# Retention and GLU feed-forward on one core: GLU blocks of 512 columns instead of 384

## The chip, the cores and the metric

The kernel runs on one core of a Trainium2 chip. The metric is the device time of one execution, in microseconds; the median of several executions is compared.

## What is computed

The reference is a retention layer (attention with a decaying mask and without softmax) followed by a feed-forward layer with a sigmoid gate. There are 8 batches and 8 heads, with 576 positions of 64 elements.

```python
scores = scale * np.matmul(q, k.transpose(0, 1, 3, 2))
gamma = 1.0 - 2.0 ** (-5.0 - np.arange(H))
Dmat = np.where(rel >= 0, gamma[:, None, None] ** rel[None, :, :], 0.0)
attn_out = np.matmul(scores * Dmat[None], v)
x = attn_out.transpose(0, 2, 1, 3).reshape(B * S, H * D)      # 4608 x 512
gate = 1.0 / (1.0 + np.exp(-(x @ w_gate)))                    # 4608 x 1536
out = (gate * (x @ w_val)) @ w_out                            # 4608 x 512
```

All inputs and the output are float32 in memory; the kernel multiplies in bfloat16 and accumulates in float32.

## The kernel before, in words

The retention is computed chunk by chunk with a running state. Its result stays on chip as xT (512 x 4608, transposed, with one column for each token), and the feed-forward reads it from there. The columns of xT come in the order in which the steps are computed. The first 768 columns come from three pairs of chunks that a start-up part handles by its own code (lines 624 to 784), together with the feed-forward of columns 0 to 511.

After that the work is in STEPS (line 68), numbered from 0: one step is one chunk of one batch, 128 columns, or 64 for the last chunk of a batch (a short step). Steps 0 to 6 end at columns 896, 1024, 1088, 1152, 1280, 1408 and 1536; steps 2 and 3 are short, steps 4, 5 and 6 are the first three chunks of batch 2.

A step is made ready by loads_to and casts_to, which call the functions at lines 98 to 107 and 244 to 292: SyncE loads v, k and q (line 105), GpSimd multiplies k and q by decay tables and writes them to qk_nat in bfloat16 (lines 252 and 262), SyncE issues a transposing DMA that makes T from qk_nat (line 289), and GpSimd casts v into vbd (line 273). qk_nat, vbd and T exist four times. On each queue these stand in the order load of step s + 1, transpose of step s, load of step s + 2 and so on; the casts of step s + 3 are emitted with the QK phase of step s (LEAD_CAST).

TensorE then works a step off in phases: st0, qk, st1, pv, each of 4 to 16 matmuls of 64 columns. "st" (line 432) adds a half chunk to the state, which DVE copies to sbd (line 438). "qk" (line 399) needs T; DVE multiplies its result with a triangular mask (line 401). "pv" (lines 418 and 420) gives the columns of xT, which ACT copies (line 422). A short step has only qk and pv, and its qk stands ahead of the pv of the step before it. The list of all phases is "order".

The feed-forward runs in BLOCKS of columns. In each block and for each of 12 slices of the 1536 hidden columns, TensorE multiplies xT with a slice of w_gate and one of w_val, four matmuls each (line 495), ACT takes the sigmoid (line 519; 509 in blocks of 256 columns), and DVE multiplies (523; 511), which gives gv. Then 12 output matmuls for each 128 columns (line 561) and a copy by ACT (line 538) give the result, which SyncE stores (line 533) nine tiles late. The PSUM pool for the GLU and output tiles has three buffers of 512 float32 columns.

The two streams are interleaved by hand. ffn_units yields after each small group of matmuls: in a block of 256 columns after each slice, in wider blocks after each gate half and each value half, and in the output part after the 4th, 8th and 12th matmul of each tile. The main loop (line 789 on) then calls advance, which runs as many attention phases as the share of the block's work that is done asks for. By the end of a block, all steps whose columns the next block reads must be done: last_step and upto (lines 581 to 586) turn the next block's last column into a place in "order". The share is spread over the block without its last 6144 columns of matmul work (3 x 2048). What stands in each engine's queue is thus the order in which the program emits it.

Of the kernel before, what the change touches and what calls it, by code (L numbers as in the profile page):

```python
# [16 lines left out]
def kernel(  # L17
# [22 lines left out]
    NT, DM = out.shape  # L40
# [489 lines left out]
    def leave():  # L530
        r, ob = stores.pop(0)
        for p0, r0, w in rows(r, P):
            nc.sync.dma_start(out[r0:r0 + w, :], ob[p0:p0 + w])
# [47 lines left out]
    def upto(s):  # L581

        return order.index(("pv", s)) + 1

    def last_step(t1):
        return max(s for s in range(NS) if at_col[s] < t1)
# [196 lines left out]
        nc.vector.memset(t, 0.0)  # L783
    casts_to(1)

    BLOCKS = [(512, 256), (768, 256)] + [(t, 384) for t in range(1024, 2560, 384)]
    BLOCKS += [(t, 512) for t in range(2560, NT, 512)]
    pieces = 0
    for w, (t0, n) in enumerate(BLOCKS):
        nxt = BLOCKS[w + 1] if w + 1 < len(BLOCKS) else None  # L790
        end = upto(last_step(nxt[0] + nxt[1])) if nxt else len(order)
# [4 lines left out]
        for cols in ffn_units(t0, n):  # L796
            gone += cols
            pieces += 1
            if stores and (nxt is None or w + 2 == len(BLOCKS) and pieces % 4 == 0):
                leave()  # L800
# [33 lines left out]
```

## Time and profile before

| what | us |
|---|---|
| median of 7 runs | 337.09 (336.85 to 337.69) |
| profiled execution | 338.22 |
| its span, first to last instruction | 336.4 |
| TensorE matmul busy | 328.7 |
| weight loads busy | 184.3 |
| GpSimd busy | 185.8 |
| ACT busy | 167.8 |
| DVE busy | 164.8 |

The profile is of one execution, which took 338.22 us; all times inside it count from the first instruction of its span. Groups of instructions by line and shape that touch the change (count, busy time, mean of one):

| line, engine, what | shape | count | busy us | mean ns |
|---|---|---|---|---|
| 495 PE, gate half | 128x256 | 96 | 14.4 | 273 |
| 495 PE, gate half | 128x384 | 192 | 39.1 | 326 |
| 495 PE, gate half | 128x512 | 192 | 49.3 | 379 |
| 519 ACT, sigmoid | 128x384 | 48 | 23.6 | 491 |
| 519 ACT, sigmoid | 128x512 | 48 | 28.7 | 597 |
| 523 DVE, product | 128x384 | 48 | 26.6 | 555 |
| 523 DVE, product | 128x512 | 48 | 33.0 | 688 |
| 561 PE, output | 128x512 | 372 | 85.5 | 379 |

The value half of line 495 has the same counts and times as the gate half. The mean duration of a matmul contains its latency, and matmuls overlap, so a duration is longer than the spacing of two in a row. In the timeline of this execution the blocks start at 55.65 (column 512), 74.42 (768) and 92.47 us (1024).

### The profile page before, as it was taken

The page shows a single profiled execution, that of the slowest core. Times are in us where ns is not written, and L with a number is a line of the kernel's source. Part 1 is how long each engine was busy: PE and PEld are TensorE (multiplying, and loading weights), DVE is VectorE, ACT ScalarE, POOL GpSimd, SP SyncE. Part 2 cuts the span into 40 slices and gives each one's busy share as a digit, 9 for nine tenths or more (in the row PEclk, how much of TensorE's full clock was granted, in tenths as well). Part 3 has the DMA queues.
Part 4 walks back from the last instruction along what each step waited for, and adds up shares of the span by engine and source line. Part 5 has one row for each costly group of instructions (what it writes and reads, how often), then busy time and mean ns, then how long its engine had stood idle before and what let it go on. Part 6 is the DMA issues. An engine that isn't in the chain of part 4 may idle for free.

```text
span 336.4 us, 7396 instructions
## 1 busy us (share of the span) xinstructions
PE 328.7 (98%) x2784; PEld 184.3 (55%) x2784; DVE 164.8 (49%) x328; ACT 167.8 (50%) x345; POOL 185.8 (55%) x327
## 2 busy tenths in 40 slices
PE   7999998999999999999999999999999999999996
PEld 3544545869666566556566655544555455444443
DVE  5745765627466455536346635642664156503320
ACT  6545635537665556355456655445545455233321
POOL 5565669688968898783448976482567500000000
PEclk9999999999999999999999999999999999999999
DMA  7999996899999999999975999599773850020002
GB/s 205 312 372 367 312 250 129 141 229 193 184 211 196 185 193 218 225 237 214 230 137 113 183 244 199 105 222 255 135 143 82 244 212 2 0 95 33 0 31 95
DMA packets 164100, 60.00 MB, mean 178 GB/s; under 512 B 144480, under 2 KB 156000, under 8 KB 164064
## 3 DMA queue, kind: packets, MB, share of 16 engines
q1 hardware_dynamic: 163920, 59.39, 83.6%
q8 instruction: 22, 0.36, 0.5%
q10 hardware_dynamic: 144, 0.13, 0.1%
q14 instruction: 14, 0.11, 0.1%
HBM read 37.75 MB, written 9.44 MB: 140 GB/s over the span
## 4 chain that ended last, share of the span: by engine, by line
PE 87%; DMA 5%; POOL 4%; DVE 2%; issue 1%; ACT 0%; SPq 0%; POOLq 0%; DVEq 0%
PE h L495 46%; PE op L561 24%; PE hg L610 3%; PE hv L610 3%; DMA wo<-in_moe_w_out_dram 2%; PE pv L420 2%; PE qk L399 2%; PE pv L418 2%; DMA T<-qk_nat 2%; PE st L432 2%; POOL qk_nat L252 1%; DMA k32p<-in_k_dram 1%; PE op L551 1%; DVE ptp L335 1%; PE idle L159 1%
## 5 line engine op out<-in xcount | busy, mean ns | idle before, releaser
L495 PE MATMUL h<-xT,wg_sb 128*128 128x384 bf16 (+2 forms) x480 | 102.8, 337 | 0.2 <-DVE gv L523 0.2
L495 PE MATMUL h<-xT,wv_sb 128*128 128x384 bf16 (+2 forms) x480 | 102.8, 337 | 0.0
L252 POOL TENSOR_TENSOR qk_nat<-k,ktab 64x256 bf16<-64x256 f32 x120 | 73.5, 612 | 41.8 <-PE st L432 27.2
L523 DVE TENSOR_TENSOR gv<-g,h 128x384 bf16<-128x384 bf16 (+1 forms) x96 | 59.7, 621 | 71.7 <-PE h L495 56.4
L561 PE MATMUL op<-wo_sb,gv 128*128 128x512 bf16 x372 | 85.5, 379 | 0.0
L519 ACT ACTIVATE g<-h 128x384 bf16<-128x384 f32 (+1 forms) x96 | 52.2, 544 | 64.9 <-PE h L495 58.3
L438 DVE CAST sbd<-st 64x256 bf16<-64x256 f32 x104 | 43.7, 420 | 45.1 <-PE st L432 42.9
L495 PEld LDWEIGHTS <-wg_sb 128*128 128x128 bf16 x480 | 43.7, 98 | 31.4 <-issue 0.4
L495 PEld LDWEIGHTS <-wv_sb 128*128 128x128 bf16 x480 | 44.1, 98 | 29.0 <-issue 0.4
L273 POOL CAST vbd<-v 64x256 bf16<-64x256 f32 x120 | 47.6, 397 | 15.8 <-PE pv L420 11.2
L561 PEld LDWEIGHTS <-gv 128*128 128x128 bf16 x372 | 34.4, 98 | 36.3
L538 ACT COPY ob<-op 128x512 f32<-128x512 f32 x33 | 19.3, 586 | 47.5 <-PE op L561 42.8
L283 ACT CAST vs<-v 64x256 bf16<-64x256 f32 x104 | 41.9, 403 | 1.6
L262 POOL TENSOR_TENSOR qk_nat<-q,qtab 128x512 bf16<-128x512 f32 (+1 forms) x34 | 35.4, 1042 | 2.6
L422 ACT CAST xT<-pv 128x512 bf16<-128x512 f32 (+1 forms) x34 | 18.2, 534 | 18.1 <-PE pv L420 18.0
L401 DVE TENSOR_TENSOR pt<-qk,tri 128x512 bf16<-128x512 f32 (+1 forms) x34 | 21.2, 625 | 6.1 <-PE qk L399 5.8
L420 PE MATMUL pv<-pt,vbd 128*128 128x64 bf16 x240 | 18.0, 193 | 0.0
L432 PEld LDWEIGHTS <-qk_nat 128*128 128x128 bf16 x208 | 13.2, 98 | 8.8
L511 DVE TENSOR_TENSOR gv<-g,h 128x256 bf16<-128x256 bf16 x24 | 10.0, 421 | 14.7 <-ACT g L509 14.4
L418 PE MATMUL pv<-T,sbd 128*128 128x64 bf16 x216 | 17.2, 193 | 0.0
L420 PEld LDWEIGHTS <-vbd 128*128 128x128 bf16 x240 | 15.2, 98 | 3.6
L418 PEld LDWEIGHTS <-sbd 128*128 128x128 bf16 x216 | 15.1, 98 | 2.5
(76 smaller groups left out, 234.1 us busy)
## 6 DMA issues: line engine op xcount, KB each, us to landing
out_dram<-ob SPq DMA_DIRECT2D x34, 256.0 KB, 2.8
v<-in_v_dram SPq DMA_DIRECT2D x26, 256.0 KB, 4.0
k<-in_k_dram SPq DMA_DIRECT2D x26, 256.0 KB, 4.6
q<-in_q_dram SPq DMA_DIRECT2D x26, 256.0 KB, 5.0
wg<-in_moe_w_gate_dram SPq DMA_DIRECT2D x12, 256.0 KB, 6.1
wv<-in_moe_w_val_dram SPq DMA_DIRECT2D x12, 256.0 KB, 5.9
wo<-in_moe_w_out_dram SPq DMA_DIRECT2D x12, 256.0 KB, 5.6
k32p<-in_k_dram SPq DMA_DIRECT2D x6, 256.0 KB, 5.6
```

Source lines behind the costliest of these rows:

```text
L252: nc.gpsimd.tensor_tensor(out=kn[half(hh), j, :, half(hh)], in0=k32[half(j), hh::2, :], in1=ktab[half(j), c, hh::2].unsqueeze(2).to_broadc ...
L262: nc.gpsimd.tensor_tensor(out=qs[0:n], in0=q32[0:n], in1=qtab[0:n, c, :].unsqueeze(2).to_broadcast([n, H, D]), op=ALU.mult)
L273: nc.gpsimd.tensor_copy(out=vb[half(hh), j, :, half(hh)], in_=v32[half(j), hh::2, :])
L283: nc.scalar.copy(out=natural["vs", s][half(hh), j], in_=loaded[s][0][half(j), hh::2, :])
L401: nc.vector.tensor_tensor(out=pt[:, :, 0:n].rearrange("p m (j t) -> p m j t", t=64), in0=qkp[:, :, 0:n].rearrange("p m (j t) -> p m j t", ...
L418: nc.tensor.matmul(pvp[:, m, half(j)], lhsT=before[:, m, :], rhs=qT[:, m, half(j)], start=True, stop=False)
L420: nc.tensor.matmul(pvp[:, m, half(j)], lhsT=vb[:, j, m, :], rhs=pt[:, m, half(j)], start=before is None, stop=True)
L438: nc.vector.tensor_copy(out=sb[half(hh), :, half(hh)], in_=st_tiles[b][half(hh)])
L495: nc.tensor.matmul(out, lhsT=w_sb[:, kc, fc * P:(fc + 1) * P], rhs=xT[:, kc, t0 + a:t0 + e], start=(kc == 0), stop=(kc == NKC - 1))
L519: nc.scalar.activation(out=g[:, 0:n], in_=h1[:, 0:n], func=AF.Sigmoid)
L523: nc.vector.tensor_tensor(out=gvs[some[0]][:, a:e], in0=g[:, 0:n], in1=h2[:, 0:n], op=ALU.mult)
L561: nc.tensor.matmul(opp, lhsT=gvs[fc][:, nb * P:(nb + 1) * P], rhs=wo_sb[:, fc, :], start=(fc == 0), stop=(fc == NFC - 1))
```

## The change

The four blocks of 384 columns that cover columns 1024 to 2559 become three blocks of 512. The blocks from 2560 on were 512 wide already; so now all blocks from 1024 on are. The two blocks of 256 columns before them stay. There are 9 blocks in place of 10. Because advance takes its goal from the next block's end, the goals of the blocks from column 768 to 2048 move with the blocks.

```diff
-    BLOCKS = [(512, 256), (768, 256)] + [(t, 384) for t in range(1024, 2560, 384)]
-    BLOCKS += [(t, 512) for t in range(2560, NT, 512)]
+    BLOCKS = [(512, 256), (768, 256)] + [(t, 512) for t in range(1024, NT, 512)]
```

## The prediction

> **What bounds the kernel now.** I read the page first: its engine line and the chain that ended last.
>
> ```profile
> PE 328.7 (98%) x2784; PEld 184.3 (55%) x2784; DVE 164.8 (49%) x328; ACT 167.8 (50%) x345; POOL 185.8 (55%) x327
> ...
> PE 87%; DMA 5%; POOL 4%; DVE 2%; issue 1%; ACT 0%; SPq 0%; POOLq 0%; DVEq 0%
> ```
>
> TensorE is busy for 98% of the span and is 87% of the chain. A busy matmul row may still hide gaps, because matmuls overlap, so next I read the chain in order of time (start, duration, what), which gives the spacing of the matmuls.
>
> ```profile
> 85.76 0.23 PE qk L399 x8
> 86.00 0.87 PE h L495 x8
> ...
> 98.12 1.95 PE h L495 x12
> ...
> 302.01 20.72 PE h L495 x96
> ```
>
> One 256-column matmul costs 0.87/8 = 109 ns, one of 384 columns 1.95/12 = 162.5 ns, one of 512 columns 20.72/96 = 215.8 ns, one 64-column attention matmul 0.23/8 = 29 ns. From about 66 us to 302 us nearly every piece in this chain has exactly these rates: TensorE is the bound, and only what it issues, or a new wait in its queue, can move the end. Its waits (engine, line, what for; total, times, longest):
>
> ```profile
> PE qk L399 <- DMA T<-qk_nat: 0.8, 2, 0.6
> ...
> PE h L495 <- DVE gv L523: 0.2, 1, 0.2
> ```
>
> The first is the one to watch. The QK matmuls of an attention step need the tile T, which SyncE's transposing DMA makes from what GpSimd has cast. At the start of the blocks, at 58 and 65 us, TensorE came to QK before T had landed. So this feed is late early in the kernel, and later it is ahead.
>
> [...] the trace shows the GLU matmuls behind the QK at 65 us starting only after it. So a QK that waits holds everything behind it. [...]
>
> **The change part by part.**
>
> (1) *Fewer, wider GLU matmuls.* Four blocks of 384 have 4 x 12 x 8 = 384 matmuls, 384 x 162.5 ns = 62.40 us. Three blocks of 512 have 3 x 12 x 8 = 288, 288 x 215.8 ns = 62.15 us. Gain 0.25 us, all on the path. The output matmuls (12 per 128 columns) and all attention matmuls keep their number and shape.
>
> (2) *Sigmoids and products.* 48 of each become 36, 491 ns to 597 ns and 555 ns to 688 ns: 23.6 to 21.5 us on ACT and 26.6 to 24.8 us on DVE. Both engines are half busy and TensorE hides them: nothing. If cover went, the first to be late would be a GLU tile's PSUM buffer, as in (4).
>
> (3) *Attention is pulled forward.* Each block must run the attention whose columns the next block reads (upto/last_step). The block at 768 had to get to column 1408, which is through step 5; now it must get to 1536, so step 6 (batch 2, third chunk) moves into it. The phases left there go from 11 to 15. There are 15 yields before the last output tile, and the pacing formula then gives exactly one phase per yield. Of step 6, four phases move: st, qk, st, pv. Their TensorE time is only moved, not added. The casts, loads and transposes are emitted with the QK phases, but their order on the GpSimd and SyncE queues up to here is unchanged (v, k, q loads, transpose, repeated), so they come no earlier. When did they come?
>
> ```profile
> 84.89 1.04 POOL L262 TENSOR_TENSOR qk_nat<-q,qtab 128x512 bf16<-128x512 f32 x1
> ```
>
> ```profile
> L289 SPq DMA_TRANSPOSE T<-qk_nat x1: 2869/2869/2869, 86.0 to 86.0; - x1
> ...
> DMA to landing us min/median/max: 4.9/4.9/4.9
> ```
>
> The first fence is GpSimd's timeline: the q cast of step 6. The second is tile T in a window of two microseconds: that step's transpose, at 85.96 in SyncE's timeline. It lands at 85.96 + 4.9 = 90.86 us. GpSimd casts steps 4, 5 and 6 nearly back to back (70.99, 76.52 and 82.17 us), so it can't be faster. Before, the QK of step 6 ran at 94.54 us, 3.7 us after the landing.
>
> Now its new place. The block starts at 74.42 us as before. Ahead of that QK stand 96 GLU matmuls (96 x 109.4 ns = 10.50 us), the first four output matmuls (0.86 us), and twelve phases: QK of step 3 0.12; PV of steps 2 and 3 2 x 0.23; steps 4 and 5 each st 0.12, qk 0.23, st 0.12, with PV 0.35 and 0.46; st of step 6 0.12; sum 2.45 us. 74.42 + 10.50 + 2.45 + 0.86 = 88.23 us. T lands 2.63 us later. **TensorE waits, and the cost is +2.63 us.** The same sum for step 4 gives 79.50 against a landing at 79.6 (74.78 + 4.8), and for step 5, once that 0.10 is waited, 83.92 against 84.4 (80.31 + 4.1): waits of 0.1 and 0.5 us. These are part of the 2.63 us, not on top, since the QK of step 6 can't start before 90.86 us in any case. The same holds for delays from the denser DVE and ACT work there: about 2 us of them would vanish in that wait.
>
> What is late next: the QKs of steps 7, 8 and 9 come, with that delay, at 97.84, 101.64 and 108.62 us (same spacings, 512 columns); their T land at 95.9, 100.4 and 106.6. No further wait; after that the distance grows to some 4 us. But had step 6 not waited, step 8 would come at 99.0 and wait 1.4 us: a floor under the cost of this part. T's landings ran from 3.1 to 6.3 us over the whole kernel; with 6.3 for step 6 the wait is 4.0 us. So 1.4 to 4.0, taken at 2.63.
>
> (4) *Stalls in the 384 blocks.* Before, the block at 2176 had to fit steps 16 to 20 into 27 us. DVE and ACT fell behind and TensorE waited for a PSUM buffer:
>
> ```profile
> 179.29 0.81 PE L495 MATMUL h<-xT,wv_sb 128*128 128x384 bf16 x4
> 180.32 0.81 PE L495 MATMUL h<-xT,wg_sb 128*128 128x384 bf16 x4 [0.21 <-DVE gv L523]
> ```
>
> Starts 1.03 us apart where four matmuls need 0.65: 0.38 us lost (0.21 of it visible as idle). Two runs of twelve, at 126.59 and 134.14, took 2.07 and 2.06 for 1.95 us: 0.23 us more. The block at 2048 now gives the same five steps 34 us, and no 512 piece of the chain is stretched. I count the 0.61 us as gained (bounds 0 and 0.61).
>
> (5) *Nothing else.* Output stores and loads keep their count; three stores instead of two leave at the first wide block, queued behind transposes that are by then early. From column 2560 on, blocks and their attention are the same.
>
> Sum: -0.25 + 2.63 - 0.61 = +1.77 us. The profiled execution took 338.22 us, of which 336.4 are span; it becomes 339.99. It lies 1.13 us above the median, 337.09; the difference carries over: **338.9 us**.
>
> **Rivals.**
> - *A smaller wait.* The transpose of step 6 lands early and step 8's floor decides: -0.25 + 1.4 - 0.61 = +0.54, 337.6 us. For: landings from 3.1 us exist. Against: with 3.1 us it lands at 89.06 and step 6 waits 0.8 us, still under the floor, but the landings of steps 4 to 9, read one by one, are 4.1 to 4.9 us. One in ten.
> - *No wait at all, faster.* If T of step 6 landed by 88.23 us and step 8's by 99.0, only the gains are left: -0.25 - 0.61, 336.2 us. Its place is the QK at line 399 in the block at 768; it decides if the feed is 2.6 us earlier there, say because loads arrive sooner and GpSimd's wait of 2.25 us for k at 67 us goes. Against: that is before the change acts, and the landing would have to take 2.3 us, under the shortest seen. 6 in 100.
> - *The wait slows the clock.* [...] Against: the clock stays 9 tenths or more in every slice, through the 0.6 us wait; no run here shows a longer one in mid-kernel. 4 in 100.
>
> **How the numbers follow.** Forecast 80 in 100, small wait 10, none 6, clock 4. About 0.2% (0.7 us) is what a measurement of this kernel can tell from no change: 336.4 to 337.8 is "same". That gives slower 0.84 (forecast and clock), same 0.10, faster 0.06. The range: low, the floor of 1.4 with both gains, 337.6. High, a wait of 4.0 and no gain from (4): -0.25 + 4.0 = +3.8, 340.9[...].
>
> **What would show it.** In the changed profile the wait of QK for T rises from 0.8 us in 2 times to about 3.4 us in 5, the longest about 2 us, ending near 90.9 us; the block at 1024 starts near 96.0 us and no wait of GLU matmuls for gv is left. The wide form has spacing 216 ns. The forecast is wrong if the transpose of step 6 is issued well before 86 us, or if waits appear in the wide blocks, where I expect none.

## The result and the profile after

The changed kernel takes 339.23 us, the median of 13 runs (338.51 to 341.62). The kernel before takes 337.26 us (336.83 to 338.4) in the 32 runs made beside them. By the medians it is slower by 1.97 us; the ratio of the means is 1.0071, with an interval of 1.0057 to 1.0086. The forecast was 338.9 us.

The 13 runs are not one cloud. In nine, the granted clock is 0.999 or 1.000 and the mean time 339.0 us; in four it is 0.995 and the mean 341.4 us. The profiled execution, 341.53 us with a span of 339.8, is one of the four. Its profile therefore shows two losses, a wait and a slower clock, and the second is not in every run.

The page after: engines, the granted clock in 40 slices, and the chain's shares.

```profile
PE 330.6 (97%) x2688; PEld 175.8 (52%) x2688; DVE 162.8 (48%) x316; ACT 166.0 (49%) x333; POOL 185.9 (55%) x327
...
PEclk9999999999899999999999999999999999999999
...
PE 72%; DMA 14%; POOL 6%; SPq 5%; issue 1%; ACT 0%; POOLq 0%
```

There are 96 fewer matmuls, but TensorE's busy time has risen from 328.7 to 330.6 us: some of the matmuls took longer. DMA's share of the chain has gone from 5% to 14%, so more of what led up to the end now runs through transfers. TensorE's waits (total, times, longest):

```profile
PE qk L399 <- DMA T<-qk_nat: 2.8, 2, 2.6
```

That is the row forecast to grow. The row of GLU matmuls waiting for gv is gone. The chain in order of time, at the new wait:

```profile
84.08 1.04 POOL qk_nat L262
85.13 0.03 POOL vbd L273
85.16 5.64 DMA T<-qk_nat
90.80 0.05 issue
90.84 0.41 PE qk L399 x8
91.25 1.21 PE op L561 x4
92.46 0.21 PE st L432 x4
92.68 1.71 PE op L561 x4
```

Read it from the top: GpSimd ends the q cast of step 6 at 85.1 us, the transpose is under way until 90.80, and QK follows at once. The forecast had that landing at 90.86. The last line is something else: four output matmuls take 1.71 us where four at 215.8 ns need 0.86. Three stretches of 3.41 us, the second of them the one between two changes of the clock, show why (stretch, length, then busy time and count of PE, PEld, DVE, ACT and GpSimd; then the granted clock, the DMA share, GB/s):

```profile
88.22:91.63 3.41, 0.82 (x12) 0.54 (x12) 1.52 (x4) 0.85 (x3) 3.14 (x6) 1.00 0.83 167
91.63:95.04 3.41, 3.41 (x27) 1.81 (x25) 1.20 (x3) 0.56 (x1) 3.07 (x6) 0.50 0.96 173
95.04:98.46 3.42, 3.42 (x20) 1.57 (x18) 0.00 (x0) 2.00 (x5) 1.46 (x5) 1.00 1.31 237
```

In the first, TensorE worked for 0.82 us only; in the second, from 91.63 us, 0.8 us after the wait ended, to 95.04, the granted clock is 0.50; in the third it is 1.00 again. At half clock PE counts as busy, here for 3.41 of 3.41 us, which is why busy time rose. On the page's 40 slices of 8.5 us it is only one "8".

The account of the two profiled executions, from the spacing of TensorE's instructions beyond their own rate:

| term | us |
|---|---|
| waits at QK and near it, after: 0.20 (58 us), 0.19, 0.34 and 2.75 (steps 4, 5, 6), 0.13 at two st | 3.61 |
| less the waits of before at 58 and 65 us: 0.75 and 0.36 | -1.11 |
| clock at half after the wait | +1.67 |
| stalls of the 384 blocks gone | -0.61 |
| fewer, wider matmuls | -0.25 |
| sum | +3.31 |
| difference of the spans, 339.8 - 336.4 | +3.4 |

### The profile page after: what moved, and what is told of

It is laid out like the page before. It is cut to its first block, busy times and chain, and to the rows that moved or that the text cites. A ratio compares the mean times of both kernels' runs of the same rounds, so it can differ in the third digit from the quotient of the medians.

```text
span 339.8 us, 7167 instructions
## 1 busy us (share of the span) xinstructions
PE 330.6 (97%) x2688; PEld 175.8 (52%) x2688; DVE 162.8 (48%) x316; ACT 166.0 (49%) x333; POOL 185.9 (55%) x327
## 4 chain that ended last, share of the span: by engine, by line
PE 72%; DMA 14%; POOL 6%; SPq 5%; issue 1%; ACT 0%; POOLq 0%
PE h L495 43%; PE op L561 22%; DMA wv<-in_moe_w_val_dram 5%; POOL qk_nat L252 3%; DMA wo<-in_moe_w_out_dram 3%; DMA k<-in_k_dram 3%; SPq L114 3%; DMA q<-in_q_dram 2%; PE qk L399 2%; PE pv L420 2%; DMA T<-qk_nat 2%; PE pv L418 2%; POOL qk_nat L262 2%; PE st L432 2%; SPq L126 1%; POOL vbd L273 1%
## 5 line engine op out<-in xcount | busy, mean ns | idle before, releaser
L495 PE MATMUL h<-xT,wg_sb 128*128 128x512 bf16 (+1 forms) x432 | 100.7, 355 | 0.0
L495 PE MATMUL h<-xT,wv_sb 128*128 128x512 bf16 (+1 forms) x432 | 100.7, 355 | 0.0
L523 DVE TENSOR_TENSOR gv<-g,h 128x512 bf16<-128x512 bf16 x84 | 57.8, 688 | 66.1 <-PE h L495 51.8
L561 PE MATMUL op<-wo_sb,gv 128*128 128x512 bf16 x372 | 86.7, 383 | 0.0
L519 ACT ACTIVATE g<-h 128x512 bf16<-128x512 f32 x84 | 50.2, 597 | 66.8 <-PE h L495 66.6
L495 PEld LDWEIGHTS <-wg_sb 128*128 128x128 bf16 x432 | 39.0, 98 | 33.7
L495 PEld LDWEIGHTS <-wv_sb 128*128 128x128 bf16 x432 | 39.6, 98 | 31.5
```

What stands on the lines that cost most here:

```text
L495: nc.tensor.matmul(out, lhsT=w_sb[:, kc, fc * P:(fc + 1) * P], rhs=xT[:, kc, t0 + a:t0 + e], start=(kc == 0), stop=(kc == NKC - 1))
L519: nc.scalar.activation(out=g[:, 0:n], in_=h1[:, 0:n], func=AF.Sigmoid)
L523: nc.vector.tensor_tensor(out=gvs[some[0]][:, a:e], in0=g[:, 0:n], in1=h2[:, 0:n], op=ALU.mult)
L561: nc.tensor.matmul(opp, lhsT=gvs[fc][:, nb * P:(nb + 1) * P], rhs=wo_sb[:, fc, :], start=(fc == 0), stop=(fc == NFC - 1))
```

## The experiments

The theory: step 6 is pulled into the block at 768, its QK comes ahead of T, and TensorE waits some 2.6 us; in some executions the wait drops the clock. The first rival: the wide blocks themselves cost time (denser use of a PSUM buffer, DVE or ACT). The second: the clock is the main loss. The third question is what makes T late: GpSimd's casts, SyncE's queue, or the DMA engines. The kernel before took 337.2 to 337.3 us beside each.

**1. The pull alone, on the kernel before.**

```diff
-        end = upto(last_step(nxt[0] + nxt[1])) if nxt else len(order)
+        end = upto(last_step(nxt[0] + nxt[1]) + (1 if t0 == 768 else 0)) if nxt else len(order)
```

> The widths of before (384), but the block at 768 must finish step 6, as in the change. If the wait of the QK of step 6 for its transposed tile is the cause: a wait of about 2.6 us at that QK, ending near 91 us, and none of the gains of the wide blocks, so about 337.3 + 2.6 = 339.9 us (ratio 1.008), with some executions near 342 where the TensorE clock falls after the wait. If the width of the blocks itself costs the time: no change, 337.3 us.

Measured: 340.12 us (339.81 to 342.15), ratio 1.0096 [1.0075, 1.0116]. TensorE's waits, then its timeline (start, duration, what; in brackets the idle time before it):

```profile
PE qk L399 <- DMA T<-qk_nat: 2.8, 3, 2.5
...
PE h L495 <- DVE gv L523: 0.2, 1, 0.2
```

```profile
87.49 1.03 PE L561 MATMUL op<-wo_sb,gv 128*128 128x512 bf16 x4
90.99 0.41 PE L399 MATMUL qk<-T 128*128 128x64 bf16 x8 [2.47 <-DMA T<-qk_nat]
```

With no block made wider, the same wait appears in the same place, the gv wait of the 384 blocks stays, and the kernel is slower by 2.9 us. That is the loss of the changed kernel without its gains, so the pull accounts for the whole of it. One of the six runs, 342.15 us, had the clock at 0.995.

**2. Wide blocks without that pull** (256 columns up to 1536, then 512).

```diff
-    BLOCKS = [(512, 256), (768, 256)] + [(t, 512) for t in range(1024, NT, 512)]
+    BLOCKS = [(t, 256) for t in range(512, 1536, 256)] + [(t, 512) for t in range(1536, NT, 512)]
```

> Blocks of 512 from column 1536, and two blocks of 256 in place of the first wide one, so that no block needs a step early. If the wait is the cause: no wait for T over 0.8 us, the gains of the wide blocks less 0.3 us for the narrower matmuls, so 337.3 - 0.6 = 336.7 us (0.998). If the wide blocks cost the time by themselves (PSUM buffers, DVE and ACT in bursts): five sixths of the loss stays, about 338.9 us.

Measured: 339.98 us (339.61 to 340.22), ratio 1.0079 [1.0067, 1.0092]. A miss. TensorE's waits:

```profile
PE st L432 <- ACT g L509: 0.9, 1, 0.9
PE st L432 <- DVE sbd L438: 0.8, 2, 0.5
PE pv L420 <- POOL qk_nat L262: 0.7, 1, 0.7
```

No QK waits for T, as expected, but the step from 256 to 512 has only been moved: the block at 1280 must now bring steps 7 to 11, 18 phases, beside the work of 256 columns. It takes 23.1 us (107.64 to 130.76), and from 109 to 127 us TensorE loses 3.5 us, for which the profile names DVE, ACT and GpSimd. It doesn't acquit the wide blocks by itself; experiment 11 does. It shows that the same jump of width elsewhere costs as much by another road.

**3. The wait filled with matmuls of no use**, so that it is not idle.

```diff
+            if s == 6:
+                fill(11)
```

The fill stands ahead of the QK phase.

> The changed kernel with 11 dummy matmuls (2.4 us) ahead of the QK of step 6, in the time in which TensorE would wait. If TensorE waits for the landing there and the clock falls because it is idle: the landing still ends the wait, so the median stays near 339.0 us, but the clock stays at 1.000 and no execution is near 341.5. If the wait isn't real idle time, the dummies add 2.4 us: 341.6 us. If the clock falls for another reason, executions near 341.5 remain.

Measured: 339.42 us (339.19 to 340.4), ratio 1.0067 [1.0053, 1.008]. The timeline of TensorE:

```profile
87.98 2.54 PE L159 MATMUL idle<-blank 128*128 128x512 bf16 x11
90.35 0.40 PE L399 MATMUL qk<-T 128*128 128x64 bf16 x8
```

The eleven fill the wait and run 0.56 us past the landing, 89.79 us, so the loss stays. All six runs have the clock at 0.999 or 1.000 and none is near 341.4 us: at full clock the kernel is still 2.2 us slower than before, so the clock isn't the main loss. Six runs against 4 of 13 prove little by themselves, so here are all kernels. Before: none of the 70 runs beside the experiments at 0.995 or less. Kernels whose longest wait in the main loop was about 1 us or less (numbers 2 to 5, 7, 8, 10, 11): none of 79. Number 6, with 1.9 us: one of six. Number 1, with 2.5 us: one of six. The changed kernel, with 2.6 us: four of 13. Number 9, with 3.1 us: five of six. The waits are those of one profiled execution of each.

The profiled execution of number 1 waited 2.47 us, nearly as long as the 2.59 us of the changed kernel's, and kept its clock: 0.999 over the whole execution, against 0.995. Why one clock fell and the other didn't isn't shown, nor how long the waits were in the runs without a trace.

**4. Loads one step further ahead**, to feed GpSimd earlier.

```diff
-            loads_to(x + (1 if x < 12 else 2))
+            loads_to(x + 2)
```

> The changed kernel with every load one step earlier on SyncE's queue in the first 12 steps. If GpSimd's waits for k (2.3 us at step 3, 0.7 at step 4, 0.2 at step 6) hold the feed back: the tile of step 6 lands 2 to 3 us earlier, the wait at its QK falls under 1 us, and the time to 336.5 to 337.2 us. If the feed is held by GpSimd's own casts, or the time is lost elsewhere: no change, 339.2 us.

Measured: 339.53 us (339.19 to 340.44), ratio 1.0071 [1.0057, 1.0086]. A miss. GpSimd's timeline, then tile T from 84 to 85 us:

```profile
80.53 1.04 POOL L262 TENSOR_TENSOR qk_nat<-q,qtab 128x512 bf16<-128x512 f32 x1
```

```profile
L289 SPq DMA_TRANSPOSE T<-qk_nat x1: 1892/1892/1892, 84.5 to 84.5; - x1
...
DMA to landing us min/median/max: 5.7/5.7/5.7
```

The q cast of step 6 ended at 81.57 us, 3.6 us sooner than in the changed kernel, but the transpose left SyncE only at 84.47 and landed at 90.12. The waits spread over three QKs (1.09, 0.96, 1.05 us) and their sum stayed. So GpSimd isn't what holds T once its loads come early, since the transpose left 2.9 us after the cast; the SyncE queue or the DMA engines behind it are.

**5. The block at 768 spreads its phases to its very end.**

```diff
-            advance(begin + min(todo, -(-todo * gone // (total - 3 * 2048))))
+            advance(begin + min(todo, -(-todo * gone // (total - (0 if t0 == 768 else 3 * 2048)))))
```

> The changed kernel, with the phases of the block at 768 spread over the whole block instead of the part before its last output tile: the QK of step 6 comes 8 output matmuls (1.7 us) later. If that QK's wait for the landing is the loss: the wait falls from 2.6 to about 0.9 us, [...]and the time falls by 1.7 us, or by 1.2 us if step 8 then waits as the floor of the forecast says: 337.5 to 338.0 us. If the loss is elsewhere: no change, 339.2 us, or slower, as the PV of step 6 now ends shortly before the block that needs it.

Measured: 338.40 us (337.53 to 338.88), ratio 1.0025 [1.0014, 1.0036]. The timeline of TensorE:

```profile
88.39 1.03 PE L561 MATMUL op<-wo_sb,gv 128*128 128x512 bf16 x4
90.43 0.41 PE L399 MATMUL qk<-T 128*128 128x64 bf16 x8 [1.01 <-DMA T<-qk_nat]
```

Two more output groups stand ahead of the same QK, and the wait falls from 2.6 to 1.0 us while the landing (90.39 us) is only 0.4 us sooner. The place of the QK sets the wait. The account of the profiled execution: 1.17 lost here, 0.45 at an st, 0.86 gained by the blocks, +0.76. That execution took 337.74 us, 0.40 above before; the median lies 1.06 above, past the upper end of what was expected, and what the other executions lose isn't shown. Step 8's QK came at 99.50 us, some 0.2 us after its T, and didn't wait.

**6. k and q loaded ahead of v.**

```diff
-        for nm, src in (("v", v), ("k", k), ("q", q)):
+        for nm, src in (("k", k), ("q", q), ("v", v)):
...
-        loaded[s] = tiles
+        loaded[s] = [tiles[2], tiles[0], tiles[1]]
```

> The changed kernel with each step's loads in the order k, q, v instead of v, k, q, since GpSimd needs k first. If GpSimd's waits for k (1.9 us at step 3, 0.7 and 0.2 us later) set when the tile of step 6 lands: each k comes 0.6 to 1.5 us sooner, the landing about 1 to 1.4 us sooner, and the time is 337.8 to 338.3 us. If SyncE's queue holds the transposes back anyway, as it did with the loads early: no change, 339.2 us.

Measured: 339.18 us (338.91 to 341.47), ratio 1.0072 [1.0046, 1.0097]. A miss. Tile T from 83.3 to 84.3 us:

```profile
L289 SPq DMA_TRANSPOSE T<-qk_nat x1: 2675/2675/2675, 83.8 to 83.8; - x1
...
DMA to landing us min/median/max: 6.5/6.5/6.5
```

The transpose left 1.4 us sooner than in the changed kernel and took 6.5 us in place of 5.6; QK still waited 1.9 us. Little of this is due to the edit. In number 3, whose loads and casts are those of the changed kernel, the transpose left at 84.45 and landed at 89.79 us, and over the profiles with an unchanged feed (before, changed, 1, 2, 3, 5, 7, 11) step 6's T landed between 89.3 and 90.9 us. Those of numbers 4 and 6, 90.12 and 90.2 us, lie within that, so neither edit shows an effect on the landing.

**7. Widths that grow in steps: 256, 384, 512.**

```diff
-    BLOCKS = [(512, 256), (768, 256)] + [(t, 512) for t in range(1024, NT, 512)]
+    BLOCKS = [(512, 256), (768, 256), (1024, 256), (1280, 384), (1664, 384)] + [(t, 512) for t in range(2048, NT, 512)]
```

> Widths that grow slowly: three blocks of 256 from 512, two of 384 from 1280, 512 from 2048. By the matmul spacings this has the GLU time of before (two blocks of 384 are one of 512 and one of 256). No block needs more steps than it can hide. If the wait for the feed is the loss and the stalls of the block at 2176 the gain: no wait for T over 0.8 us, no stall of GLU matmuls for gv, 337.2 - 0.6 = 336.6 us (0.998). If wide blocks are slow in themselves: at or above 337.2 us.

Measured: 337.71 us (337.48 to 338.22), ratio 1.0009 [1.0001, 1.0017]. The timeline of TensorE:

```profile
98.41 0.28 PE L432 MATMUL st<-vs,qk_nat 128*128 128x64 bf16 x4 [0.28 <-POOL qk_nat L252]
...
104.14 0.28 PE L432 MATMUL st<-vs,qk_nat 128*128 128x64 bf16 x4 [0.28 <-DVE sbd L438]
```

No QK waits for T and no GLU matmul for gv. The loss of the wide kernel is gone, but the gain didn't come: st loses 0.45 and 0.44 us in the third block of 256, which has to fit three full steps. The time is above the 337.2 us that was to speak against wide blocks, but the profile has no wait in a block of 512.

**8. Number 7, with the phases of the first block rounded down**, so that the QKs at 58 and 65 us come later.

```diff
-            advance(begin + min(todo, -(-todo * gone // (total - 3 * 2048))))
+            advance(begin + min(todo, (todo * gone if t0 == 512 else todo * gone + total - 3 * 2048 - 1) // (total - 3 * 2048)))
```

> As the gradual widths, and the phases of the first block (column 512) rounded down instead of up, so that the QKs of steps 0 and 1 come one to two slices later, after their tiles have landed. If a QK that comes too early costs what it waits: the waits of up to 0.8 and 0.4 us at 58 and 65 us go as well, 336.6 - 1.0 = 335.6 us (0.995). If the waiting is only moved: 336.6 us.

Measured: 337.74 us (337.38 to 338.39), ratio 1.0013 [1.0005, 1.0021], the same as number 7. A miss with a lesson: in the profile of number 7 T landed at 56.58 and 62.06 us and nothing waited at 58 or 65 us. In the seven profiles with the start and feed of before (changed, 1, 2, 3, 5, 7, 11) TensorE loses 0.20 us there at most, and 1.11 us in the profile of before. So these waits belong to that one execution, and most likely not to the kernel's median.

**9. The loads of v on ACT's queue**, with the earlier loads of number 4.

```diff
-            nc.sync.dma_start(out=t[0:n], in_=src[b, :, t0:t0 + n, :].rearrange("h p d -> p h d"))
+            queue = nc.scalar if nm == "v" and 2 <= s <= 8 else nc.sync
+            queue.dma_start(out=t[0:n], in_=src[b, :, t0:t0 + n, :].rearrange("h p d -> p h d"))
```

> The changed kernel with the loads one step early, and the v loads of steps 2 to 8 issued from ACT's queue. With the loads early alone, GpSimd was no longer late, yet the tile of step 6 landed only 0.6 us sooner, near 90.2 us. If SyncE's queue holds the transposes back: it has a quarter less to issue for each step, the transpose of step 6 is issued 1 to 2 us sooner, and the time falls to 337.5 to 338.5 us. If the DMA engines are the limit: the landing stays near 90 us and the time near 339.3 us, or more, as ACT is delayed by the issues.

Measured: 342.46 us (339.94 to 343.45), ratio 1.0134 [1.011, 1.0158]. TensorE's wait, then two stretches of 3.41 us (columns as above):

```profile
PE h L496 <- DVE gv L512: 3.1, 1, 3.1
```

```profile
60.81:64.22 3.41, 1.03 (x13) 0.78 (x11) 0.22 (x1) 0.99 (x3) 3.10 (x6) 1.00 1.31 189
64.22:67.63 3.41, 2.71 (x25) 2.13 (x25) 2.32 (x6) 1.13 (x4) 3.16 (x6) 0.50 1.23 210
```

ACT computed nothing from 59.04 to 63.19 us. Its next issue of a v load came at 62.74, and its cast of v (line 284) and the sigmoids stood behind it. The profile puts the 4.15 us down to the landing of a v; what held the issue isn't shown. So DVE was late with gv, TensorE stood idle from 61.8 to 64.9 us, and the granted clock was 0.50 from 64.22 to 67.63 us. T of step 6 left at 84.64 and landed at 89.9 us (90.12 in number 4), but with such a stall ahead of it this doesn't answer what the experiment was made for. It is a second trace in which half clock comes with a long idle wait, here of 3.1 us.

**10. The v loads of steps 2 to 8 left out**, the k tile used in their place, with the earlier loads of number 4.

```diff
+            if nm == "v" and 2 <= s <= 8:
+                continue
...
-        loaded[s] = tiles
+        loaded[s] = tiles if len(tiles) == 3 else [tiles[0]] + tiles
```

> As the loads one step early, and the v loads of steps 2 to 8 are left out (k's tile is used in their place, so a third of the input of these steps isn't read). SyncE has as little to issue as with v on ACT's queue, and the DMA engines move a third less. If the DMA engines limit the feed: the tile of step 6 lands 2 us or more sooner, only here and not with v on ACT's queue, and the time falls to about 337 us. If SyncE's queue does: both fall alike. If GpSimd's casts do (5.5 us for each step): neither falls below 338.5 us.

Measured: 337.28 us (336.88 to 337.99), ratio 1.0001 [0.9993, 1.0009]. Tile T from 81.3 to 82.3 us, then TensorE's timeline:

```profile
L291 SPq DMA_TRANSPOSE T<-qk_nat x1: 1457/1457/1457, 81.7 to 81.7; - x1
...
DMA to landing us min/median/max: 3.8/3.8/3.8
```

```profile
84.78 0.28 PE L434 MATMUL st<-vs,qk_nat 128*128 128x64 bf16 x4 [0.28 <-POOL qk_nat L254]
...
88.09 0.40 PE L401 MATMUL qk<-T 128*128 128x64 bf16 x8
...
89.64 0.28 PE L434 MATMUL st<-vs,qk_nat 128*128 128x64 bf16 x4 [0.30 <-DVE sbd L440]
```

The q cast ended at 81.66 us, 0.1 later than in number 4, but the transpose left at once and landed at 85.46, 4.7 us sooner than in number 4. QK of step 6 runs at 88.09 without a wait. With fewer loads in the queue and on the DMA engines the same change costs next to nothing. And what the waits for T had covered comes to light: st loses 0.23 us at 80.03, 0.44 at 84.78 and 0.46 at 89.64, the last two behind GpSimd and DVE. -0.25 - 0.61 + 1.13 = +0.27. The profiled execution, 337.48 us, lies 0.25 above before; the median lies 0.05 above. Leaving the loads out relieves SyncE's queue and the DMA engines together; number 9 was to relieve the queue alone and was spoilt, so the share of each stays open.

**11. 384 up to column 1792, then 512, and 256 at the end.**

```diff
-    BLOCKS = [(512, 256), (768, 256)] + [(t, 512) for t in range(1024, NT, 512)]
+    BLOCKS = [(512, 256), (768, 256), (1024, 384), (1408, 384)] + [(t, 512) for t in range(1792, 4352, 512)] + [(4352, 256)]
```

> The start of before (256, 256, 384, 384), then five blocks of 512 from 1792 and one of 256 at the end; the matmul spacings give the same GLU time as before. No block needs a step earlier than before did up to column 1408, and the dense block at 2176 is gone. If wide blocks only cost when their predecessor can't hide the steps they need: as fast as before or faster, by the stalls of the 384 blocks (up to 0.6 us): 336.7 to 337.3 us. If width itself costs: slower, 338 us or more.

Measured: **336.73 us** (336.47 to 336.85), ratio 0.998 [0.9972, 0.9989], faster than both kernels. TensorE's waits begin with the start-up part's:

```profile
PE idle L159 <- DVE blank L152: 1.3, 1, 1.3
PE kTp L311 <- POOL kp L242: 0.9, 1, 0.9
```

No line of QK, st or GLU in the main loop stands in that view; from 54 to 300 us matmuls lose about 0.1 us in all. T of step 6 landed at 89.72 us and its QK came at 93.81. The GLU matmuls cost as much as before (192 x 162.5, 480 x 215.8 and 96 x 109.4 ns are 145.3 us, against 145.3 for 384 x 162.5 and 384 x 215.8), so the 0.50 us gained fits the stalls of before, 0.61 us in the forecast, all of which have gone from the profile: the one in the block at 2176 and also the two in the block at 1408, which is still 384 wide but is followed by a block of 512. What the 256 block at the end does to the tail isn't separated from it.

## Why the prediction was right

The time lay 0.3 us above the forecast, inside the range, and the place and the cause were as told. That it lay so near is partly luck, as the steps show:

- **(1) Fewer, wider matmuls, -0.25 us.** Held. The chain has the wide form at the same spacing, 20.72/96 = 215.8 ns:

```profile
305.39 20.72 PE h L495 x96
```

- **(2) Sigmoids and products, nothing.** Held: no wait on ACT or DVE in a wide block of the changed kernel.
- **(3) The pull, +2.63 us.** The mechanism held, and experiments 1, 5 and 10 show it from three sides: the pull alone brings it, a later place of the QK shrinks it, an earlier T removes it. The size: the nine runs at full clock average 339.0 us, 1.74 us above before; with the two gains, -0.25 and -0.61, that leaves 2.6 us for the waits. In the profiled execution the steps were 0.19, 0.34 and 2.75 us, where 0.1, 0.5 and 2.0 were forecast. The wait view has 2.8 us in 2 waits, the longest 2.6, where about 3.4 in 5 with a longest of 2 were forecast. The landing was forecast at 90.86 and was 90.80, but partly by luck: everything came 0.8 us sooner (block at 74.42, in fact 73.58; transpose at 85.96, in fact 85.16), and the transpose took 5.64 us and not 4.9. The block at 1024 started at 97.64 us, not near 96.0; without the clock's 1.67 us that is 95.97. One reading was wrong: GpSimd "can't be faster". With the loads early its q cast of step 6 ended 3.6 us sooner (experiment 4).
- **(3), the delays that "would vanish in that wait".** They were put at about 2 us. Experiment 10, without the wait, shows 1.1 us of them. The idea held; the size was too large.
- **(3), the floor of 1.4 us from step 8.** Not borne out, and not tested by itself. In no profile did step 8's QK wait for T. The forecast put the landing at 100.4 us, as in the kernel before; in the changed kernel it was 99.63, and 97.01 in experiment 10, which took the pressure from all steps at once. Experiment 5 comes nearest: QK at 99.50, some 0.2 us after the landing.
- **(4) Stalls of the 384 blocks, -0.61 us.** Held: the gv line is gone, and experiment 11, with the stalls gone and the pull not made, gained 0.50 us.
- **(5) Nothing else.** This is the term that failed: it left no room for the clock, which was kept among the rivals.
- **The clock, 4 in 100.** That the wait slows the clock was right, its chance was far too low: it came in 4 of 13 runs, on top of the forecast wait, and cost 1.67 us in the profiled execution. The argument against it was that no wait of before was longer than 0.6 us and the clock stayed; that says nothing of a wait of 2.6 us. Four traces have waits of 1.9 us and more: the clock fell to half with 2.59 us (the changed kernel) and 3.1 us (experiment 9) and stayed full with 1.9 us (experiment 6) and 2.47 us (experiment 1). The two groups of runs lie 2.4 us apart, and the clock explains 1.67 of it. The waits of the profiled execution, 3.61 us in all, are 1.0 us above the 2.6 us of the nine others, so the four may also be those whose T came latest; that is argued from one profile. One run of number 6 took 341.13 us at full clock beside four of 338.9 to 339.3, so 2 us more can come without the clock; of what isn't shown.
- **"The difference carries over"** from the profiled execution to the median. It didn't quite: 1.1 us of waits at 58 and 65 us in the profile of before are most likely not in most executions (experiment 8), which the longer landing happened to offset.

## What to carry to other kernels

Where two streams are interleaved by hand, a block's width also sets how much of the other stream the block before it must hide. Compare each block with its successor: from 256 straight to 512 a step is pulled ahead of its data. Here 256, 256, 384, 384, 512 kept the gain from the stalls and none of the wait (experiment 11), while a third block of 256 ahead of the 384s gave the gain back (experiment 7). Before such a change, take the landing time of each feed from the trace, work out where its reader will stand, and count an idle wait on TensorE as long as the 2.59 us here twice: once for itself and once for the clock, which fell in 4 of the 13 runs here and cost 1.67 us in the profiled one.

## What was not expected of the hardware

- In the profiled execution TensorE's clock fell to half 0.8 us after a wait of 2.59 us and was full again 3.41 us later: output matmuls 427 ns apart in place of 216, a loss of 1.67 us. In experiment 9 it was at half for 3.41 us, from 64.22 us, with a wait from 61.8 to 64.9 us. In experiment 1 it stayed full with a wait of 2.47 us.
- The transposing DMA of one step (step 6) landed in 3.8 us with the v loads left out and in 4.6 to 6.5 us beside them. Nothing else that was tried on the loads moved its landing out of the 89.3 to 90.9 us that it has without a change to them.
- Moving seven loads to ACT's queue came with a stall of TensorE of 3.1 us, by way of a late sigmoid and product.
